# Value groups taken head by head, an earlier end for jobs, and a shorter limit for VectorE's units in an attention and gated-layer kernel

## The chip, the cores and the metric

The kernel runs on one core of a Trainium2 chip. The core has five engines that run their own instruction queues in order and meet through semaphores: TensorE (matmuls; in the profile PE, its weight loads PEld), VectorE (DVE), ScalarE (ACT), GpSimd (POOL) and SyncE (SP), which here issues the DMA transfers. Matmul results go to PSUM, a small memory of banks that hold 512 32-bit numbers in each of 128 partitions; everything else lies in SBUF or in the chip's main memory. The metric is device time of one execution in microseconds (us), lower is better; the time shown is the median of the runs.

## The reference

Two pre-norm blocks follow each other on 2048 rows of 640 numbers: 32-head attention with heads of 20 numbers, then a gated bilinear layer of width 1728. Inputs and output are bf16.

```python
def _A_ref(x, wqkv, wo):
    H = 32; Dh = D // H                    # D = 640, Dh = 20
    qkv = (x @ wqkv).reshape(B, S, 3, H, Dh).transpose(2, 0, 3, 1, 4)
    q, k, v = qkv[0], qkv[1], qkv[2]
    scores = jnp.einsum("bhqd,bhkd->bhqk", q, k) * (Dh ** -0.5)
    p = _softmax(scores, axis=-1)
    o = jnp.einsum("bhqk,bhkd->bhqd", p, v)
    return o.transpose(0, 2, 1, 3).reshape(B, S, D) @ wo
...
def _B_ref(x, w_gate, w_up, w_down):
    g = jnp.einsum("bsd,df->bsf", x, w_gate)
    u = jnp.einsum("bsd,df->bsf", x, w_up)
    return jnp.einsum("bsf,fd->bsd", g * u, w_down)
...
h = x + _A_ref(_layernorm(x), A_wqkv, A_wo)
h2 = h + _B_ref(_layernorm(h), B_w_gate, B_w_up, B_w_down)
```

## The kernel before

**Units and tiles.** Scores are made transposed: keys in the partitions, queries along the row. The smallest piece is a unit: one head, 128 keys, 512 queries (256 in the last passes, "A" and "B"). Four heads form a group; a segment is one group with all its keys for one block of queries (in the first block, a quarter of the keys). The list `segs` (lines 302 to 313) orders the segments, and units of consecutive segments are packed, head after head within a block of 128 keys, into 683 tiles of 1536 columns, three PSUM banks. With 256 queries, two blocks of keys of one head stand next to each other in that list.

**What is done with a tile.** `emit_S` (line 438) writes a tile's scores with TensorE into one of two score buffers of PSUM (`sc`, matmuls of line 448) and has ScalarE write exp of them into one of six buffers `E` (line 461). A score matmul uses 32 rows of TensorE's array, so that four heads lie in four bands of rows. Two tiles later `emit_AV` (line 586) multiplies the exponentials with the values (line 615): each unit writes 32 partitions of one accumulator bank, one column band of the array for each of the four heads, so four units of different heads can run beside each other. Call four such units a step. A column of ones in the values makes the sums for softmax. When a segment's last unit is in, VectorE copies the accumulator (line 626 or 631) and `norm` or `job_norm` divides by the sums, with several small DMAs (lines 530 to 541) or on TensorE.

**VectorE's units.** Where VectorE has time, `emit_x` (line 478) gives the last 512 columns of a tile to it: line 486 reads them from PSUM, and four more operations (lines 496, 497, 498, 491) make an approximate exponential `xe` in integer arithmetic. ScalarE's instruction on that tile is then 1024 columns wide. `x_takes` (line 472) decides it; one of its conditions is that the tile is at least `X_LEAST` tiles ahead of the segment's last. The four operations wait in `x_pieces` until `spare` (line 412) finds room for them, and `put_x` (line 502) then sets the unit at the end of its segment's part of the queue `av_q`. `need_x` makes what is missing before a segment ends.

**How a value group is taken.** `emit_AV` is called once a tile. It counts units at the head of `av_q` that are of one segment and at least two tiles old, eight at most (sixteen narrow ones). With fewer it returns, unless the oldest is over three tiles older than that. It then takes them in the order of the queue.

**Jobs, and the planner that sets the order.** All other work of TensorE (projections, line 278; values, line 292; transposes, line 260; output projection, line 830; gate and up, lines 896 and 914; down, line 951) is cut into jobs, generators that yield after each matmul with its cost. The order of every engine is fixed when the program is built. The main loop (line 1121) goes over the tiles: scores of the tile, one value group, events that are due, then jobs by `run_job` (line 429). It keeps account of times in `at`: TensorE (`pe`), VectorE (`dve`), the job bank `mi`, ScalarE's end (`exp`), the score buffers (`slot`). `S_NS` is the cost of a tile's scores, `S_EXP` the time from scores to the earliest start of the exponential, `SWITCH` what a change of work costs. A value group is charged one step of `w * 5 // 12` ns for every four units. `run_job` is given the time at which TensorE must be free for the next scores; it begins a job only if the job's first part fits, and goes on while the next 216 ns fit, with 60 ns over:

```python
run_job(max(at["exp"] - S_EXP, at["slot"][-2]))
...
while at["pe"] + 216 <= until + 60:
    if step() in (None, NEXT, END):
        break
```

All jobs share one PSUM bank `mi`, which VectorE empties. If there are no jobs, `keep_warm` (line 424) puts two matmuls of no use (line 427) in the gap. What is left of the last block of queries runs in `last_tail` (line 1031) after the last exponential.

**Line numbers.** The changed file is the same up to line 600 and two lines longer from the middle of `emit_AV` on; below, lines are those of before.

Of the kernel before, what the change touches and what calls it, by code (L numbers as in the profile page):

```python
# [27 lines left out]
HPG = 4  # L28
# [3 lines left out]
QB = 512  # L32
# [20 lines left out]
WARM = 58  # L53
LAG = 10
EXP_NS, EXP_END, EXP_COL = 50, 166, 5 / 6
S_NS, S_EXP, SWITCH, LAT = 323, 445, 110, 150
TOL, LEAST = 200, 430
X_LEAST, X_OUT = 4, 6
SHIFT = 1184.0
LOG2E = 1.4426950408889634  # L60
X_UNIT = 128.0
# [10 lines left out]
def kernel(  # L72
# [154 lines left out]
    at = {"pe": 0, "dve": 0, "mi": 0, "acc": 0, "slot": [0, 0], "exp": 0, "av": {}}  # L227
# [88 lines left out]
    for s, (p, g, lo, hi, _) in enumerate(segs):  # L316
        w = PASS[p][2]
# [111 lines left out]
    def run_job(until):  # L429
        if cur["fresh"]:  # L430
            key = urgent[0][0] if urgent else cur["key"] if cur["gen"] is not None else jobs[0][0] if jobs else None
            if key is None or max(at["pe"], at["mi"]) + SWITCH + COST.get(key[0], LEAST) > until:
                return
# [3 lines that stand above are left out]
# [149 lines left out]
    def emit_AV(upto):  # L586
        put_x()
        if not av_q:
            return
        if acc["seg"] is not None and av_q[0][1] != acc["seg"]:  # L590
            need_x(acc["seg"])
            put_x()
        i, s = av_q[0][0:2]
        p, g, lo, hi, kind = segs[s]
        b, c0, w = PASS[p]
        if acc["seg"] != s:
            if at["pe"] < at["acc"] and now["i"] < acc["from"]:
                return
            acc["seg"], acc["left"], acc["n"] = s, (hi - lo) * HPG, [0] * HPG
            acc["t"] = accp.tile([P, QB], F32, name="acc")  # L600
        most = 2 * HPG * QB // w
        ready = 0
        for u in av_q:
            if u[0] > upto or u[1] != s or ready == most:
                break
            ready += 1
        if ready < min(most, acc["left"]) and i > upto - 3:
            return
        for _ in range(ready):
            _, _, kt, j, e = av_q.popleft()  # L610
            if (s, kt, j) in x_last:
                x_live["units"] -= 1
            ensure(("v", kt, g // (NG // 2)))
            h = HPG * g + j
            nc.tensor.matmul(  # L615
                acc["t"][SLOT * j:SLOT * (j + 1), 0:w],
                lhsT=vx[kt][:, VS * h:VS * h + SLOT], rhs=e,
                start=(acc["n"][j] == 0), stop=(acc["n"][j] == hi - lo - 1))
            acc["n"][j] += 1
        acc["left"] -= ready  # L620
        at["pe"] += SWITCH + -(-ready // HPG) * w * 5 // 12
        if acc["left"] == 0:
            dve(690)
            if kind in ("copy", "only"):
                asb = parts[g] if kind == "copy" else nrm.tile([P, QB], F32, name="asb")
                nc.vector.tensor_copy(asb[:, 0:w], acc["t"][:, 0:w])
                if kind == "copy":
                    part[g] = asb
            else:
                asb = part[g]  # L630
                nc.vector.tensor_tensor(asb[:, 0:w], acc["t"][:, 0:w], asb[:, 0:w], ALU.add)
            acc["seg"], acc["from"], at["acc"] = None, now["i"] + 2, at["dve"] + LAT
            if s == FINAL:
                final["asb"] = asb
            elif (p, g) in FAST:
                urgent.append((("nf", p, g), job_norm(s, asb)))
            elif kind in ("only", "last"):
                norm(s, asb)
# [482 lines left out]
    while i < n_tiles or av_q:  # L1121
        now["i"] = i
        if i < n_tiles:
            emit_S(i)
        else:
            while step_x():
                pass
        if i == first_last:
            for g in range(NG):
                ensure(("spill", g))  # L1130
            load_res()
        if i == n_tiles:
            root = small.tile([P, 1], BF16, name="root")
            nc.scalar.activation(root[:], ones[:], ACT.Sqrt)
        emit_AV(i if i >= n_tiles else i - 2 if i >= LAG else i - 4)
        run_events(i)
        if b_seen < NB - 1 and normed(str(b_seen), range(NG)):
            add_tail(b_seen, list(range(TPB)))
            b_seen += 1
        if not a_seen and normed("3", range(SPLIT_G)) and normed("A", range(SPLIT_G, NG)):  # L1140
            add_tail(LAST_B, [0, 1])
            a_seen = True
        if i < n_tiles:
            run_job(max(at["exp"] - S_EXP, at["slot"][-2]))
            idle = max(at["pe"], at["mi"]) + SWITCH + 2 * BANK * EXP_COL / 2
            if i > WARM and cur["gen"] is None and not jobs and idle < at["slot"][-2] + TOL:
                keep_warm()
                at["pe"] = idle
            spare(max(at["pe"], at["slot"][-2]))
        i += 1  # L1150
# [103 lines left out]
```

## Time and profile before

| what | before |
|---|---|
| median of three runs | 979.75 us (979.02 to 979.91) |
| the profiled execution | 976.79 us |
| its span, first to last instruction | 974.9 us |
| mean granted TensorE clock | 0.967 |
| ScalarE busy | 909.5 us |
| TensorE busy | 857.6 us |
| VectorE busy | 589.7 us |

The profile is of one execution. A row of a group gives line, engine, operation, output and input tile, count, then busy time in us and mean length in ns, then the engine's idle time ahead of these instructions with what ended it. Busy time counts overlapping instructions once, so that it can be less than count times mean. The ends of matmuls are modelled: one starts before the other's end. "PEclk" is the share of full clock that TensorE was granted, in tenths. A row of a timeline has start, length, engine, line, and count of a run of like instructions without a gap.

### The profile page before, as it was taken

What the parts mean: (1) busy time and instruction counts of PE and PEld (TensorE: products, weight loads), DVE (VectorE), ACT (ScalarE), POOL (GpSimd) and SP (SyncE); (2) the same over time, 40 slices, a digit from 0 to 9 for tenths busy, and PEclk for the clock granted to TensorE, in tenths of its full rate; (3) what the DMA queues carried; (4) which work ended last, traced back from release to release, by engine and by line L of the source; (5) the groups of instructions that cost most, each with busy time, mean ns of one, the idle gap of its engine ahead of it and who ended that gap; (6) DMA issues with size and microseconds to landing.
All of it is one profiled execution on the core that took longest, in us unless ns stands there. A gap on an engine that the chain in (4) does not pass through costs nothing.

```text
span 974.9 us, 18079 instructions
## 1 busy us (share of the span) xinstructions
PE 857.6 (88%) x7219; PEld 334.2 (34%) x7219; DVE 589.7 (60%) x1181; ACT 909.5 (93%) x719; POOL 65.4 (7%) x163
## 2 busy tenths in 40 slices
PE   7888989888988899988898989988889989988887
PEld 5233232222233222422232223332332334444455
DVE  7665357777777777768777777787562331243232
ACT  6899999999999999999999999999999999999951
POOL 3120011200000000000000000000000000000000
PEclk9999999999987999989997999999998999979999
DMA  6000010100150221041021230001502001202310
GB/s 183 28 2 1 1 37 12 42 17 13 39 156 4 66 67 33 27 149 63 11 64 33 66 88 13 26 27 30 138 2 66 14 13 27 61 8 64 84 34 17
DMA packets 67817, 44.44 MB, mean 46 GB/s; under 512 B 18504, under 2 KB 63404, under 8 KB 67728
## 3 DMA queue, kind: packets, MB, share of 16 engines
q1 hardware_dynamic: 67728, 43.23, 16.0%
q8 instruction: 58, 0.95, 0.4%
q14 instruction: 31, 0.25, 0.1%
HBM read 35.91 MB, written 7.30 MB: 44 GB/s over the span
## 4 chain that ended last, share of the span: by engine, by line
PE 43%; ACT 32%; issue 15%; DVE 9%; DMA 1%; POOL 0%; ACTq 0%; SPq 0%; DVEq 0%; POOLq 0%
ACT E L461 32%; PE sc L448 10%; PE acc L615 8%; PE mi L896 6%; PE mi L278 5%; PE mi L951 5%; PE mi L830 2%; PE f L896 2%; PE mi L292 1%; PE mi L427 1%; PE mi L914 1%; DVE qa L285 1%; PE f L951 1%; DVE u L247 1%; DVE hh L904 1%
## 5 line engine op out<-in xcount | busy, mean ns | idle before, releaser
L461 ACT ACTIVATE E<-sc 128x1536 bf16<-128x1536 f32 (+1 forms) x683 | 892.2, 1411 | 26.0 <-PE sc L448 18.5
L448 PE MATMUL sc<-qa,kT 32*128 32x512 bf16 x1536 | 204.5, 392 | 45.9 <-ACT E L461 41.8
L615 PE MATMUL acc<-E,vx 128*32 128x512 bf16 (+1 forms) x2336 | 186.2, 361 | 0.5 <-ACT E L461 0.5
L448 PEld LDWEIGHTS <-kT 32*128 32x128 bf16 x2432 | 79.5, 91 | 287.1 <-issue 253.4
L486 DVE TENSOR_SCALAR xv<-sc 128x512 f32<-128x512 f32 x95 | 65.5, 690 | 55.3 <-PE sc L448 54.3
L278 PE MATMUL mi<-lnT,wp 128*128 128x512 bf16 x310 | 83.5, 384 | 14.3 <-DVE qa L285 6.4
L547 POOL TENSOR_TENSOR on<-asb,bc 128x512 bf16<-128x512 f32 (+1 forms) x30 | 35.5, 1185 | 726.8 <-DMA bc<-scr 518.0
L448 PE MATMUL sc<-qb,kT 32*128 32x256 bf16 (+1 forms) x896 | 70.9, 300 | 14.5 <-ACT E L461 13.6
L615 PEld LDWEIGHTS <-vx 128*32 128x32 bf16 x2432 | 54.5, 96 | 76.4 <-issue 64.1
L497 DVE SCALAR_TENSOR_TENSOR xt<-xm 128x512 f32<-128x512 int32 x95 | 67.1, 706 | 2.1
L951 PE MATMUL mi<-wd,hh 128*128 128x320 bf16 x378 | 65.9, 301 | 2.3 <-DVE xr L955 2.3
L491 DVE SCALAR_TENSOR_TENSOR xe<-xt,xv 128x512 int16<-128x512 f32 x95 | 67.1, 706 | 1.2
L498 DVE SCALAR_TENSOR_TENSOR xt<-xt,xm 128x512 f32<-128x512 f32 x95 | 66.4, 699 | 2.2
L247 DVE CAST u<-mi 128x512 bf16<-128x512 f32 (+1 forms) x42 | 29.0, 690 | 42.0 <-PE mi L896 41.7
L427 PE MATMUL mi<-kT,ident 128*128 128x512 bf16 x178 | 54.2, 386 | 0.0
L951 PEld LDWEIGHTS <-hh 128*128 128x128 bf16 x448 | 39.3, 97 | 38.8 <-issue 26.2
L896 PE MATMUL mi<-ln2T,wu 128*128 128x512 bf16 (+1 forms) x170 | 48.5, 400 | 3.9 <-DVE hh L904 3.9
L896 PE MATMUL mi<-ln2T,wg 128*128 128x512 bf16 (+1 forms) x170 | 45.7, 381 | 5.9 <-DVE u L247 5.8
L496 DVE TENSOR_SCALAR xm<-xv 128x512 int32<-128x512 int32 x95 | 49.3, 519 | 0.6
L904 DVE TENSOR_TENSOR hh<-mi,u 128x512 bf16<-128x512 f32 (+1 forms) x42 | 28.9, 687 | 32.7 <-PE mi L896 32.4
L278 PEld LDWEIGHTS <-wp 128*128 128x128 bf16 x310 | 26.6, 97 | 57.6 <-issue 41.0
L955 DVE TENSOR_TENSOR xr<-mi,xr 128x320 bf16<-128x320 f32 x27 | 13.1, 485 | 49.0 <-PE mi L951 49.0
(150 smaller groups left out, 637.1 us busy)
## 6 DMA issues: line engine op xcount, KB each, us to landing
bc<-scr SPq DMA_DIRECT2D x100, 64.0 KB
wu<-in_B_w_up_dram SPq DMA_DIRECT2D x20, 320.0 KB
wg<-in_B_w_gate_dram SPq DMA_DIRECT2D x20, 320.0 KB
qsp<-qa SPq DMA_DIRECT2D x8, 384.0 KB
xr<-in_A_x_dram SPq DMA_DIRECT2D x16, 160.0 KB
out_dram<-xr SPq DMA_DIRECT2D x14, 160.0 KB
wd<-in_B_w_down_dram SPq DMA_DIRECT2D x13, 160.0 KB
xs<-in_A_x_dram SPq DMA_DIRECT2D x3, 640.0 KB
```

Source lines behind the costliest of these rows:

```text
L278: nc.tensor.matmul(ps[:], lhsT=wslice(m, g, c), rhs=lnT[:, c, ch * QB:(ch + 1) * QB], start=(c == 0), stop=(c == KT - 1))
L427: nc.tensor.matmul(ps[:], lhsT=ident[:], rhs=kT[0][:, 0:BANK], start=True, stop=True)
L448: nc.tensor.matmul(sc[:, o:o + w], lhsT=kT[g][SLOT * j:SLOT * (j + 1), kt * P:(kt + 1) * P], rhs=q_of(g, b, c0, w)[SLOT * j:SLOT * (j + 1) ...
L461: exps = nc.scalar.activation(e[:, 0:n_act], sc[:, 0:n_act], ACT.Exp, bias=EXP_BIAS, scale=SM_SCALE)
L486: took = nc.vector.tensor_scalar(v[:], ps, X_SCALE, X_BASE, ALU.mult, ALU.max)
L491: nc.vector.scalar_tensor_tensor(e[:], t[:], X_C, v[:], ALU.add, ALU.add)
L496: (480, lambda: nc.vector.tensor_scalar(m[:], v[:].bitcast(I32), 0x7FFF, 0x8000, ALU.bitwise_and, ALU.bitwise_or)),
L497: (700, lambda: nc.vector.scalar_tensor_tensor(t[:], m[:], X_A, m[:], ALU.mult, ALU.mult)),
L498: (700, lambda: nc.vector.scalar_tensor_tensor(t[:], t[:], X_B, m[:], ALU.add, ALU.mult)),
L615: nc.tensor.matmul(acc["t"][SLOT * j:SLOT * (j + 1), 0:w], lhsT=vx[kt][:, VS * h:VS * h + SLOT], rhs=e, start=(acc["n"][j] == 0), stop=(ac ...
L896: nc.tensor.matmul(ps[0:M, 0:n], lhsT=st["w", fp][k][:, c, f2 * P:f2 * P + M], rhs=st["ln2T"][:, c, c0:c0 + n], start=(c == 0), stop=(c == ...
L951: nc.tensor.matmul(ps[:, 0:HALF], lhsT=st["hh"][f][0:K, t * P:(t + 1) * P], rhs=late["Wd"][f][0:K, cs], start=(f == 0), stop=(f == 2 * FP ...
```

## The change

It has three parts.

- The value group is taken from the whole part of the queue that is old enough: at most two units of each head (four of each in the narrow passes), the first of every head, then the second, and so on. The count is the sum over the heads, and the rule on waiting with fewer than the full number is as before.
- `S_EXP` is 500 in place of 445, and `run_job` is given a time that is another 100 ns (`MARGIN`) earlier, if the score buffer is not free even later.
- `X_LEAST` is 3 in place of 4.

```diff
-S_NS, S_EXP, SWITCH, LAT = 323, 445, 110, 150
-TOL, LEAST = 200, 430
-X_LEAST, X_OUT = 4, 6
+S_NS, S_EXP, SWITCH, LAT = 323, 500, 110, 150
+TOL, LEAST, MARGIN = 200, 430, 100
+X_LEAST, X_OUT = 3, 6
...
-        most = 2 * HPG * QB // w
-        ready = 0
+        most, rows = 2 * HPG * QB // w, [[] for _ in range(HPG)]
         for u in av_q:
-            if u[0] > upto or u[1] != s or ready == most:
+            if u[0] > upto or u[1] != s:
                 break
-            ready += 1
+            if len(rows[u[3]]) < most // HPG:
+                rows[u[3]].append(u)
+        ready = sum(len(r) for r in rows)
         if ready < min(most, acc["left"]) and i > upto - 3:
             return
-        for _ in range(ready):
-            _, _, kt, j, e = av_q.popleft()
+        for u in [r[k] for k in range(most // HPG) for r in rows if k < len(r)]:
+            av_q.remove(u)
+            _, _, kt, j, e = u
...
-            run_job(max(at["exp"] - S_EXP, at["slot"][-2]))
+            run_job(max(at["exp"] - S_EXP - MARGIN, at["slot"][-2]))
```

## The prediction

> **What bounds the kernel now.** I read the page first: busy shares, granted clock, the chain of waits that ended last.
>
> ```profile
> span 974.9 us, 18079 instructions
> PE 857.6 (88%) x7219; PEld 334.2 (34%) x7219; DVE 589.7 (60%) x1181; ACT 909.5 (93%) x719; POOL 65.4 (7%) x163
> PEclk9999999999987999989997999999998999979999
> PE 43%; ACT 32%; issue 15%; DVE 9%; DMA 1%; POOL 0%; ACTq 0%; SPq 0%; DVEq 0%; POOLq 0%
> ```
>
> ScalarE has the most work, yet the chain spends 43% of the span on TensorE and 32% on ScalarE. So ScalarE's exponentials (line 461) set the pace, and TensorE makes them late. How much is late follows from the groups by shape and ScalarE's timeline (start, length, count in a merged run).
>
> ```profile
> L461 ACT ACTIVATE E<-sc 128x1536 bf16<-128x1536 f32 x587 | 811.1, 1470 | 23.8 <-PE sc L448 17.5 <-PE acc L615 2.6
> L461 ACT ACTIVATE E<-sc 128x1024 bf16<-128x1024 f32 x96 | 100.8, 1050 | 2.2 <-PE sc L448 1.0
> ...
> 802.97 4.14 ACT L461 ACTIVATE E<-sc 128x1536 bf16<-128x1536 f32 x3
> ...
> 16.02 4.14 ACT L461 ACTIVATE E<-sc 128x1536 bf16<-128x1536 f32 x3 [0.66 <-PE sc L448]
> ...
> 914.71 18.82 ACT L461 ACTIVATE E<-sc 128x1536 bf16<-128x1536 f32 x14
> ```
>
> One exponential lasts 1.47 us, but it overlaps the next: three in a row take 4.14, so one starts (4.14 - 1.47) / 2 = 1.33 after the other. The narrow form, with a bank given to VectorE, lasts 0.42 less, so its spacing is 0.91. Without a stall the 683 would take 587 x 1.33 + 96 x 0.91 = 868.1 us. They run from 16.02 to 914.71 + 18.82 = 933.53, which is 917.5. So **49.4 us are stalls**. The busy column hides this: the idle time shown is 26.0, because an exponential that starts late within the overlap leaves no idle gap.
>
> The list of waits (total us, times, longest) and the chain in order of time (start, length) say whose fault it is.
>
> ```profile
> ACT E L461 <- PE sc L448: 18.5, 38, 1.5
> ...
> ACT E L461 <- PE acc L615: 2.6, 2, 1.7
> ```
>
> ```profile
> 411.29 0.39 PE sc L448 x3
> 411.69 0.75 PE acc L615 x8
> 412.44 0.65 PE mi L951 x4
> 413.09 0.32 PE sc L448 x3
> 413.41 1.19 PE mi L951 x8
> 414.60 0.32 PE sc L448 x3
> 414.93 0.55 PE acc L615 x8
> ...
> 422.44 0.65 PE mi L951 x4
> 423.09 0.37 PE sc L448 x3
> ...
> 423.51 0.94 ACT E L461
> ```
>
> For 12 us the chain goes scores, value products, job matmuls, scores (and, in the lines left out, twice VectorE's copy of a job's bank): TensorE never waits for a free score buffer, and the exponential at 423.51 starts when its scores arrive. I went through all 682 starts: 200 are late by over 20 ns and carry 46.8 of the 49.4 us; the rest are late by 20 ns or less. In none of the 200 had TensorE begun the scores within 0.13 us of the buffer's release. All 200 are thus TensorE behind the written order. 103 of them are late by at most 0.155 us; 24, by over 0.4 us, carry 21.0.
>
> **The change, part by part.** The margin first. S_EXP goes from 445 to 500 and MARGIN takes off 100, so a job must end 0.155 us earlier before the next scores. S_EXP stands for the time from scores to exponential. TensorE's timeline has the scores of that late tile at 423.02, the exponential started at 423.51, so 0.49:
>
> ```profile
> 423.02 0.39 PE L448 MATMUL sc<-qa,kT 32*128 32x512 bf16 x3
> ```
>
> The new 500 is right and 445 was short. If each of the 200 gets its scores 0.155 earlier, 23.7 of the 46.8 remain: 23.1 removed.
>
> Then the value products. A group of eight units ran in queue order; a unit that VectorE took is missing there, so one head can come three times.
>
> ```profile
> 411.62 0.82 PE L615 MATMUL acc<-E,vx 128*32 128x512 bf16 x8
> ...
> 414.86 0.41 PE L615 MATMUL acc<-E,vx 128*32 128x512 bf16 x4
> 415.08 0.38 PE L615 MATMUL acc<-xe,vx 128*32 128x512 bf16 x1
> 415.09 0.39 PE L615 MATMUL acc<-E,vx 128*32 128x512 bf16 x3
> ```
>
> The first group took 0.82; the second ended at 415.09 + 0.39, 0.62 after it began. Three steps against two: 0.20 a step. The planner charges eight units as two steps always, so each long group puts TensorE 0.20 behind. In the order of the built programs, 106 groups need over two steps before and none after; in steps of full width 627 fall to 545, and the groups rise from 262 to 281. That is 82 x 0.20 = 16.4 us of TensorE less, and 19 group changes more at 0.12 each (chain: 0.55 for a group of two steps less 2 x 0.215), 2.3. It counts only where it made scores late: 71 of the 200 have such a group since TensorE's last wait. Less 0.20 on these alone removes 10.5; margin and grouping together leave 18.9 of 46.8, so 27.9 removed. That is the upper end, for the work cut from one tile goes into another. The lower end is grouping alone, 10.5. I take 24, near the upper end, since all 200 fit the mechanism.
>
> In the narrow passes (256 columns, the last quarter of the run) pairs of one head stood next to each other, and now alternate.
>
> ```profile
> 803.47 0.63 PE L615 MATMUL acc<-E,vx 128*32 128x256 bf16 x16
> ```
>
> Sixteen end 0.63 after the first begins. A matmul lasts 0.28, so 0.35 lies between the first and last start: three intervals of 0.11, hence four steps already, as many as after. Nothing is gained. The Trainium skill (TensorE: Matmul & The Clock Gate, Part 3, "What overlaps and what doesn't") says matmuls start strictly in program order; by that the pairs would have made nine steps, and the change would save about 5 x 0.11 in each of 48 groups, 26 us of TensorE. The row shows four, so by the trace the saving is 0.
>
> VectorE's units: X_LEAST 3 and the earlier TensorE times let 102 be taken, not 95. Each takes 0.42 from ScalarE: 7 x 0.42 = 2.9 off.
>
> ```profile
> L497 DVE SCALAR_TENSOR_TENSOR xt<-xm 128x512 f32<-128x512 int32 x95 | 67.1, 706 | 2.1
> L491 DVE SCALAR_TENSOR_TENSOR xe<-xt,xv 128x512 int16<-128x512 f32 x95 | 67.1, 706 | 1.2
> L498 DVE SCALAR_TENSOR_TENSOR xt<-xt,xm 128x512 f32<-128x512 f32 x95 | 66.4, 699 | 2.2
> L486 DVE TENSOR_SCALAR xv<-sc 128x512 f32<-128x512 f32 x95 | 65.5, 690 | 55.3 <-PE sc L448 54.3
> L496 DVE TENSOR_SCALAR xm<-xv 128x512 int32<-128x512 int32 x95 | 49.3, 519 | 0.6
> L615 PE MATMUL acc<-xe,vx 128*32 128x512 bf16 (+1 forms) x96 | 36.4, 390 | 0.0
> ...
> 115.00:690.00 575.00, 513.87 (x3758) 170.43 (x3755) 425.31 (x765) 561.81 (x441) 36.16 (x31) 0.97 0.18 49
> ```
>
> A unit costs VectorE 3.32 us, seven cost 23.2. The last row is a window (TensorE, weight loads, VectorE, ScalarE, GpSimd busy): VectorE is idle for 150 of 575 us there, which covers them. Where the cover fails, an operation stands ahead of a job's copy out of PSUM: 0 to 7 x 0.7 = 4.9 lost. I take 1.0.
>
> New waits. Holding units back for their head keeps an E buffer longer. In the built order four more exponentials (tiles 176, 240, 283, 432) wait for a value group that TensorE gets only after their own scores; behind such an exponential the next score buffer is freed late. The row "ACT E L461 <- PE acc L615" has 2.6 in two such, longest 1.7: 0 to 6.8. Scores and group take 0.32 + 0.55 against the 0.49 that scores alone need, some 0.4 late at most if ScalarE has no lead, so I take 0.3 each, 1.2.
>
> The tail. Jobs end later, and four more matmuls of line 951 come after the last exponential, 1.19 / 8 = 0.15 each: 0.6, or 0 if they lie beside VectorE's copy of the accumulator. I take 0.6. Head and tail are otherwise the same.
>
> DMAs. None is added. On SP's queue three pairs of weight loads, one spill and some stores now stand behind a few transfers of sums and reciprocals that stood behind them; nobody waits for the spill or the stores, and GpSimd's queue is unchanged. The weights are loaded two tiles ahead, and the trace has one wait for them:
>
> ```profile
> L914 PE MATMUL mi<-ln2T,wu 128*128 128x256 bf16 x30 | 4.7, 275 | 3.9 <-DVE hh L921 2.6 <-DMA wu<-in_B_w_up_dram 1.3
> ```
>
> 0 to 3 x 1.3 = 3.9; I take 0, as that one is of the last block and the moved ones are not.
>
> Fillers. The matmul pairs of line 427 fall from 89 to 65, since jobs spread over more tiles.
>
> ```profile
> L427 PE MATMUL mi<-kT,ident 128*128 128x512 bf16 x178 | 54.2, 386 | 0.0
> ...
> 304.00:314.00 10.00, 9.05 (x48) 2.72 (x47) 6.97 (x23) 9.65 (x8) 0.00 (x0) 0.50 0.01 3
> ...
> 300.30:303.70 3.40, 2.09 (x22) 0.77 (x22) 2.79 (x10) 3.40 (x4) 0.00 (x0) 1.00 0.00 0
> ...
> 440.00:450.00 10.00, 8.88 (x65) 2.62 (x63) 7.15 (x12) 10.00 (x9) 0.00 (x0) 1.00 0.20 73
> ```
>
> The first window shows the clock at 0.50 (third column from the end) with TensorE recorded 9.05 of 10 us busy and neither job nor filler in it; just ahead of it TensorE was busy 2.09 of 3.40; the third, with fillers, has 1.00. Over the run 61 us went at half clock, and 8.0 of the stalls lie there, 0.13 per us. If all 24 tiles that lose a filler fell to half clock, 24 x 1.33 x 0.13 = 4.2 would be lost. The stretches without job or filler stand at nearly the same places in both orders, so I take 0. The Trainium skill (same page, Part 1, "The HAM clock gate") halves the clock after an idle window of about 3.4 us. The window ahead of 304 is far from idle and the clock fell, so by that rule no dip would be there, before or after; the row decides against it.
>
> **The sum.** 24 + 2.9 - 1.0 - 1.2 - 0.6 = 24.1 us off. The profiled execution took 976.79 us (span 974.9 and 1.9 around it): 952.7. The median of the runs, 979.75, lies 3.0 above that execution, so by the median **955**, rounded down from 955.7. With all terms at their good ends 27.9 + 2.9 = 30.8, so 949; at their bad ends 10.5 + 2.9 - 4.9 - 6.8 - 0.6 - 3.9 - 4.2 = -7.0, so 987, but these have no reason to fall together.
>
> **The rivals.**
> *Only the grouping pays.* The margin moves a job's matmuls to the next tile, which then ends at its own limit. For: jobs hold most tiles, TensorE is busy 513.87 of 575. Against: 89 pairs of fillers are slack. 10.5 + 2.9 - 2.8 = 10.6 off: 969.
> *Nearly all lateness goes.* Late tiles follow each other, so what is put right once helps the next. Then the stalls at half clock (8.0) and the first ones (3.6 before tile 20) remain, 11.6 of 49.4: 37.8 + 2.9 - 2.8 = 37.9 off, 942. Against: the 24 that are late by over 0.4, which 0.155 doesn't cure.
> *The narrow groups pay after all* (in-order pairs): of the 11.0 us of stalls in those passes the margin leaves 4.6 (the same subtraction there), and these would go as well: 28.7 off, 951. The row of sixteen speaks against it. (This is the rule of order of the Trainium skill's page TensorE: Matmul & The Clock Gate, above.)
> *Slower: TensorE waits for VectorE's units.* They are now taken into a group as soon as their head is short, and up to three tiles from a segment's end; scores stand behind that matmul in the queue. It decides from 24.1 / 102 = 0.24 us a unit on; at 0.35 each, 35.7 lost, the time is 991. Against: idle before "acc<-xe" is 0.0 over 96 now, and a unit must still be two tiles old.
> *It does nothing that shows*: stalls come back elsewhere, 979.
>
> **How the numbers follow.** Forecast 0.70, grouping alone 0.11, nearly all 0.08, narrow groups 0.02, slower 0.06, nothing 0.03. The forecast's own range is 949 to 963, from the good end to half the margin's gain; for 8 in 10 I go from 944, toward the case of 942, to 969, the case of grouping alone. A measurement of this kernel tells about 0.2%, 2 us, from no change: faster 0.91, same 0.03, slower 0.06.
>
> **What would show it.** Right: exponentials' stalls of 22 to 30 us by the same sum; a last exponential that ends near 910; value groups of eight never over 0.65; 103 narrow exponentials; idle before "acc<-xe" at 0. Margin wrong: late tiles still near 200 and most job chains unbroken. Fillers wrong: more than two more zones at 0.50. Wrong altogether: "acc<-xe" or "E <- acc" with over 7 us of idle.

## The result and the profile after

| | before | after |
|---|---|---|
| median of 18 runs | 978.75 us (975.91 to 981.44) | 974.9 us (968.01 to 978.13) |
| ratio of the times | | 0.9959, 95% interval 0.9945 to 0.9973 |
| the profiled execution | 976.79 us | 973.8 us |
| mean granted TensorE clock in it | 0.967 | 0.954 |

The change makes the kernel 0.4% faster: 3.9 us by the medians, where 24.1 were forecast. The time lies above the forecast's range. (The forecast started from 979.75, the median of the first three runs of before; over all 18 it is 978.75.)

The page of the profile after, span, busy shares, granted clock and the engines of the chain that ended last:

```profile
span 972.0 us, 17983 instructions
PE 842.6 (87%) x7171; PEld 323.9 (33%) x7171; DVE 606.6 (62%) x1216; ACT 900.9 (93%) x719; POOL 66.3 (7%) x163
PEclk9999999899988799997997999999887999979999
ACT 40%; PE 33%; issue 15%; DVE 10%; POOL 1%; DMA 1%; SPq 0%; ACTq 0%; POOLq 0%; DVEq 0%
```

TensorE's busy time fell by 15.0 us, and the chain has 33% of the span on it in place of 43%. Most of the 15.0 is the fillers of line 427, which had 54.2 us before:

```profile
L427 PE MATMUL mi<-kT,ident 128*128 128x512 bf16 x130 | 39.8, 388 | 0.0
```

The value groups got shorter too. Their matmuls outside the stretches at half clock, scaled to all units, are 184.3 us of TensorE before and 170.1 after: 14.2 less, which is the 16.4 less 2.3 that were worked out. More time at half clock (below) hides part of it in the busy column. The span fell by 2.9 only, so most of what TensorE was spared came back as waiting. The groups by shape and ScalarE's timeline (line 617 is line 615 of before) give the stalls by the prediction's own sum:

```profile
L461 ACT ACTIVATE E<-sc 128x1536 bf16<-128x1536 f32 x580 | 803.7, 1514 | 22.6 <-PE sc L448 17.3 <-PE acc L617 3.7
L461 ACT ACTIVATE E<-sc 128x1024 bf16<-128x1024 f32 x103 | 113.2, 1099 | 7.8 <-PE sc L448 6.9 <-PE acc L617 0.5
```

```profile
15.54 10.89 ACT L461 ACTIVATE E<-sc 128x1536 bf16<-128x1536 f32 x8 [0.66 <-PE sc L448]
...
880.00 48.60 ACT L461 ACTIVATE E<-sc 128x1536 bf16<-128x1536 f32 x36 [0.34 <-PE sc L448]
```

Without a stall, 580 x 1.33 + 103 x 0.91 = 865.1 us. They run from 15.54 to 928.60, which is 913.1, so 48.0 us are stalls, against 49.4 before. The forecast had 22 to 30. The list of waits shows of what kind they are now:

```profile
ACT E L461 <- PE sc L448: 24.2, 29, 4.8
ACT E L461 <- PE acc L617: 4.2, 4, 1.7
```

Before, 38 waits for scores had 18.5 us and the longest was 1.5. Now 29 have 24.2 and the longest is 4.8. Sorted by how late each exponential starts after the one ahead of it (in us; the spacings are taken to the nanosecond, so the totals differ a little from the sum above):

| stalls of | before | after |
|---|---|---|
| up to 0.06 | 4.4 | 3.3 |
| 0.06 to 0.15 | 6.3 (61 tiles) | 3.8 (39) |
| 0.15 to 0.4 | 17.7 (73) | 10.6 (48) |
| over 0.4 | 21.0 (24) | 30.5 (24) |
| total | 49.4 | 48.2 |
| tiles late by over 0.02 | 200 | 136 |

The small stalls shrank by 10.7 us, and the large ones grew by 9.5. Two make that up, 5.04 us behind the exponential that starts at 183.18 and 4.39 us behind the one at 53.50; before, the largest of all was 1.88.

**The stall at 183.** The timeline of after there (start, length, engine, line, operation, count, idle time ahead with what ended it):

```profile
180.64 1.27 POOL L547 TENSOR_TENSOR on<-asb,bc 128x512 bf16<-128x512 f32 x1 [25.29 <-DMA bc<-scr]
181.11 5.65 DVE L496 TENSOR_SCALAR xm<-xv 128x512 int32<-128x512 int32 x1
...
181.84 4.63 POOL L774 MEMSET wo<- 128x640 bf16 x8
...
186.68 0.73 DVE L285 TENSOR_SCALAR kT<-mi,one_row 128x512 bf16<-128x512 f32 x1
...
187.47 1.44 PE L278 MATMUL mi<-lnT,wp 128*128 128x512 bf16 x3 [4.70 <-DVE kT L285]
...
188.84 0.61 PE L448 MATMUL sc<-qa,kT 32*128 32x512 bf16 x3
...
189.55 1.02 ACT L461 ACTIVATE E<-sc 128x1024 bf16<-128x1024 f32 x1 [4.83 <-PE sc L448]
```

Line 496, one of the four operations of VectorE's unit, has a median of 0.42 us, and lasts up to 1.5 where it begins inside another line 547. Here it began while GpSimd was in line 547 and stood until GpSimd's eight memsets (the clearing of the output weights' tiles in `load_wo`, line 774) were over. Behind it on VectorE waited the copy of a projection out of the job bank, behind that the next job on TensorE, behind that the scores. The same place before:

```profile
181.36 0.42 DVE L496 TENSOR_SCALAR xm<-xv 128x512 int32<-128x512 int32 x1
181.79 1.27 POOL L547 TENSOR_TENSOR on<-asb,bc 128x512 bf16<-128x512 f32 x1 [28.11 <-DVE xm L496]
181.81 1.80 DVE L497 SCALAR_TENSOR_TENSOR xt<-xm 128x512 f32<-128x512 int32 x1
183.00 4.64 POOL L772 MEMSET wo<- 128x640 bf16 x8
...
186.99 0.92 DVE L496 TENSOR_SCALAR xm<-xv 128x512 int32<-128x512 int32 x1
```

Before, line 496 ended just ahead of line 547, and the next one came near the end of the memsets. It was line 497 that began inside line 547, and it lasted 1.80 in place of 0.69, but ended well ahead of the memsets' end. The change moved VectorE's unit by 0.9 us against GpSimd's work: from 0.43 ahead of line 547's start to 0.47 behind it.

**The stall at 53.5.** TensorE's timeline of after, and behind it that of before at the same tile (the 27th):

```profile
52.35 0.39 PE L448 MATMUL sc<-qa,kT 32*128 32x512 bf16 x3 [0.63 <-ACT E L461]
...
53.46 0.85 PE L292 MATMUL mi<-wv,lnT 128*128 128x320 bf16 x5
54.95 0.84 PE L292 MATMUL mi<-wv,lnT 128*128 128x320 bf16 x5 [0.64 <-DVE vx L247]
56.38 1.24 PE L278 MATMUL mi<-lnT,wp 128*128 128x512 bf16 x5 [0.58 <-DVE vx L247]
57.55 0.39 PE L448 MATMUL sc<-qa,kT 32*128 32x512 bf16 x2
58.75 0.40 PE L448 MATMUL sc<-qa,kT 32*128 32x512 bf16 x4 [0.81 <-DVE kT L285]
```

```profile
54.33 1.25 PE L278 MATMUL mi<-lnT,wp 128*128 128x512 bf16 x5
55.51 0.39 PE L448 MATMUL sc<-qa,kT 32*128 32x512 bf16 x2
56.42 0.39 PE L448 MATMUL sc<-qa,kT 32*128 32x512 bf16 x4 [0.52 <-DVE kT L285]
```

The third of this tile's scores (the first of the x4) waits for the copy of a projection of keys (line 278), which must be made by then, whether it fits or not (`ensure` in `emit_S`). Before, that projection alone stood ahead. With the margin jobs were put off, and now two value jobs (line 292) and the projection stand between two tiles' scores, each waiting for VectorE to empty the one job bank.

### The profile page after: what moved, and what is told of

Its sections match the earlier page's. It is cut to its first block, busy times and chain, and to the rows that moved or that the text cites. A ratio compares the mean times of both kernels' runs of the same rounds, so it can differ in the third digit from the quotient of the medians.

```text
span 972.0 us, 17983 instructions
## 1 busy us (share of the span) xinstructions
PE 842.6 (87%) x7171; PEld 323.9 (33%) x7171; DVE 606.6 (62%) x1216; ACT 900.9 (93%) x719; POOL 66.3 (7%) x163
## 4 chain that ended last, share of the span: by engine, by line
ACT 40%; PE 33%; issue 15%; DVE 10%; POOL 1%; DMA 1%; SPq 0%; ACTq 0%; POOLq 0%; DVEq 0%
ACT E L461 40%; PE sc L448 8%; PE acc L617 6%; PE mi L898 4%; PE mi L278 4%; PE mi L953 3%; PE f L898 2%; PE mi L832 1%; DVE st L182 1%; PE mi L292 1%; DVE xm L496 1%; PE f L953 1%; DVE kT L285 1%; DVE u L247 1%; DVE xt L498 1%
## 5 line engine op out<-in xcount | busy, mean ns | idle before, releaser
L461 ACT ACTIVATE E<-sc 128x1536 bf16<-128x1536 f32 (+1 forms) x683 | 883.3, 1451 | 30.4 <-PE sc L448 24.2
L448 PE MATMUL sc<-qa,kT 32*128 32x512 bf16 x1536 | 208.2, 396 | 56.0 <-ACT E L461 47.5
L617 PE MATMUL acc<-E,vx 128*32 128x512 bf16 (+1 forms) x2330 | 175.2, 365 | 0.4 <-ACT E L461 0.4
L486 DVE TENSOR_SCALAR xv<-sc 128x512 f32<-128x512 f32 x102 | 70.2, 688 | 39.4 <-PE sc L448 38.2
L498 DVE SCALAR_TENSOR_TENSOR xt<-xt,xm 128x512 f32<-128x512 f32 x102 | 72.7, 713 | 2.1
L497 DVE SCALAR_TENSOR_TENSOR xt<-xm 128x512 f32<-128x512 int32 x102 | 72.0, 706 | 2.4
L491 DVE SCALAR_TENSOR_TENSOR xe<-xt,xv 128x512 int16<-128x512 f32 x102 | 71.1, 697 | 1.1
L617 PEld LDWEIGHTS <-vx 128*32 128x32 bf16 x2432 | 45.2, 96 | 69.4 <-issue 68.8
L898 PE MATMUL mi<-ln2T,wu 128*128 128x512 bf16 (+1 forms) x170 | 49.4, 400 | 5.9 <-DVE hh L906 5.7
L278 PEld LDWEIGHTS <-wp 128*128 128x128 bf16 x310 | 26.0, 97 | 59.3 <-issue 43.5
L832 PE MATMUL mi<-wo,on 128*128 128x320 bf16 x224 | 39.1, 307 | 1.5 <-DVE xr L836 1.3
L617 PE MATMUL acc<-xe,vx 128*32 128x512 bf16 x102 | 39.4, 405 | 0.8 <-DVE xe L491 0.8
```

Of the source, the lines that this page charges most:

```text
L278: nc.tensor.matmul(ps[:], lhsT=wslice(m, g, c), rhs=lnT[:, c, ch * QB:(ch + 1) * QB], start=(c == 0), stop=(c == KT - 1))
L448: nc.tensor.matmul(sc[:, o:o + w], lhsT=kT[g][SLOT * j:SLOT * (j + 1), kt * P:(kt + 1) * P], rhs=q_of(g, b, c0, w)[SLOT * j:SLOT * (j + 1) ...
L461: exps = nc.scalar.activation(e[:, 0:n_act], sc[:, 0:n_act], ACT.Exp, bias=EXP_BIAS, scale=SM_SCALE)
L486: took = nc.vector.tensor_scalar(v[:], ps, X_SCALE, X_BASE, ALU.mult, ALU.max)
L491: nc.vector.scalar_tensor_tensor(e[:], t[:], X_C, v[:], ALU.add, ALU.add)
L497: (700, lambda: nc.vector.scalar_tensor_tensor(t[:], m[:], X_A, m[:], ALU.mult, ALU.mult)),
```

## The experiments

My theory after reading the two traces: groups and X_LEAST give what was forecast, and the margin loses it again through the order it makes, at these two places. The rivals: the half clock, which rose from 63.6 us of the span to 89.5, costs it; or the grouping doesn't pay. Twelve kernels were run. Times are medians; "before" is the kernel before on the same chip in the same series.

| run | median us | before | ratio, 95% interval |
|---|---|---|---|
| e4_memset_spread | 976.06 | 978.17 | 0.9984 (0.996 to 1.0008) |
| e5_fill_waits | 973.72 | 978.17 | 0.996 (0.9934 to 0.9986) |
| e6_early_as_before | 979.32 | 978.17 | 1.0005 (0.9984 to 1.0027) |
| e8_all | 977.88 | 978.17 | 1.0001 (0.9971 to 1.003) |
| k1_memset_vector | 970.49 | 978.05 | 0.9912 (0.9881 to 0.9942) |
| f1_no_margin | 968.24 | 978.05 | 0.9895 (0.9871 to 0.9918) |
| k7_no_groups | 989.65 | 978.05 | 1.0105 (1.0077 to 1.0133) |
| k3_charge_all | 965.11 | 978.05 | 0.9873 (0.9848 to 0.9897) |
| p1_margin_late | 966.52 | 977.1 | 0.9889 (0.9851 to 0.9927) |
| p0_no_margin_late | 967.9 | 977.1 | 0.9912 (0.9884 to 0.994) |
| p4_charge_fill | 960.63 | 977.1 | 0.983 (0.9793 to 0.9867) |
| g3_xleast_alone | 975.26 | 977.1 | 0.9985 (0.9966 to 1.0005) |

Margin or grouping alone upon the kernel before were not tried. In several of the orders that follow a value group would, with six `E` buffers, wait for an exponential that itself waits for that group; these have seven, and where a run has seven this is said.

**e4: the memsets one to a tile.**

```diff
-        for g in range(NG):
+        def one(g):
             nc.gpsimd.memset(wo[g][:], 0.0)
-        for g in range(NG):
             for j in range(HPG):
                 ...
+        for g in range(NG):
+            later(g, lambda g=g: one(g))
```

> The changed kernel, with GpSimd's eight memsets of wo (and the loads behind each) put one to a tile instead of all eight at once; nothing else moves on TensorE, VectorE and ScalarE. Theory A (the margin and the groups gain as reckoned, and the gain is lost in a few places: one VectorE operation of 5.65 us beside the memsets, more time at half clock, and an early tile): the longest operation of line 496 falls from 5.65 to under 2 us, the gap of 5.0 us between exponentials near 183 us goes, and the time falls by 5 to 7 us, to 968 to 970. Theory B (the lateness is set by VectorE having more to do, and comes back elsewhere): the block goes but the time falls by less than 2 us.

The edit didn't do what it was made for. The timeline of this run:

```profile
183.83 1.27 POOL L547 TENSOR_TENSOR on<-asb,bc 128x512 bf16<-128x512 f32 x1 [25.21 <-DMA bc<-scr]
184.16 5.80 DVE L496 TENSOR_SCALAR xm<-xv 128x512 int32<-128x512 int32 x1
...
185.04 4.64 POOL L774 MEMSET wo<- 128x640 bf16 x8
```

The memsets were issued over eight tiles, but GpSimd's queue stood in order behind line 547, which waits for a DMA, and when that came they ran in one go as before. Line 496 stood 5.80 us. Nothing on the price follows, except that the same meeting gives the same stall again (5.18).

**e5: filler matmuls in every tile in which no job ran.**

```diff
+            pe_was = at["pe"]
             run_job(max(at["exp"] - S_EXP - MARGIN, at["slot"][-2]))
 ...
-            if i > WARM and cur["gen"] is None and not jobs and idle < at["slot"][-2] + TOL:
+            if i > WARM and cur["fresh"] and at["pe"] == pe_was and idle < at["slot"][-2] + TOL:
```

> The changed kernel, with the pair of filler matmuls (line 427) in every tile in which no job ran, not only when no job is left: 108 pairs for 65. Theory A: time at half clock falls from 92 us to under 20, the stalls inside such stretches from 20 us to under 8 (the 5 us beside the memsets stay), and the time falls by 7 to 11 us, to 964 to 968. Theory B: the half clock goes, but the fillers make scores late in their place and the time falls by less than 3 us, or rises.

The groups of this run have 216 filler matmuls in place of 130, and the time at half clock fell from 89.5 to 45.1 us:

```profile
L427 PE MATMUL mi<-kT,ident 128*128 128x512 bf16 x216 | 67.1, 393 | 3.5 <-DVE on L580 1.8 <-DVE sums_all L564 0.7 <-DVE ln2T L247 0.7
```

The ratio is that of the change itself (0.996 and 0.9959), the medians differ by 1.2 us, and the stalls are 46.8 against 48.2. The spans of the two profiled executions differ by 3.0, as the tail is shorter too (below). So 44 us less of half clock, bought with 86 more filler matmuls, are worth 0 to 3 us, and the expected 7 to 11 didn't come. That is not the price of the half clock alone, since fillers and the order that they make can cost something too: in the two traces the stalls fall by 4.9 us between tiles 87 and 511 and rise by 3.1 behind them. The runs of one kernel point to a higher price. Take as time at half clock twice what the granted clock lacks of 1, times the span: the 48 runs of before in the series of this table had 58 to 80 us of it, and in each of the three series a run is about 0.3 us longer for each us more (0.28 to 0.31). By that figure the 26 us that after has more than before would be some 8 us; that the clock is the cause there was not tested. The rival thus can't account for all of the 20 us that are missing, and for a part of them it stays open.

**e6: the job limit of before up to tile 86.** Both places lie ahead of tile 125.

```diff
-            run_job(max(at["exp"] - S_EXP - MARGIN, at["slot"][-2]))
+            run_job(max(at["exp"] - (S_EXP + MARGIN if i > 86 else 445), at["slot"][-2]))
```

> The changed kernel, with the old limit for jobs (445, no margin) up to tile 86, where projections are due before scores. Theory A: the gap of 4.4 us near 53 us falls to 1.6 as before, and the time by 2 to 3 us, to 972. Theory B: no change within 1 us. The orders after tile 86 can shift, so the collision with the memsets may go or come with it, worth 5 us.

A miss. `emit_S` still reckons with `S_EXP` 500 when it sets `at["exp"]`, so the planner's times stayed other than before (p1 below changes that place too), and the projection still came late: the stall near 55 us was 4.10, that at the memsets 5.19.

**e8: the edits of e4, e5 and e6 together.**

```diff
-            nc.gpsimd.memset(wo[g][:], 0.0)
+            later(g, lambda g=g: one(g))
 ...
-            run_job(max(at["exp"] - S_EXP - MARGIN, at["slot"][-2]))
+            run_job(max(at["exp"] - (S_EXP + MARGIN if i > 86 else 445), at["slot"][-2]))
 ...
+            if i > WARM and cur["fresh"] and at["pe"] == pe_was and idle < at["slot"][-2] + TOL:
```

> The three edits of the other runs together (memsets one to a tile, fillers in every tile without a job, old limit up to tile 86) on the changed kernel. Theory A: 15 to 20 us off, 955 to 960, which is what the prediction reckoned with for the change alone. Theory B: 970 or more.

Since neither place was mended (3.62 us near 57 and 5.19 near 191), it shows no gain either. It says nothing on the price of the two.

**k1: the memsets on VectorE, one to a tile.** This takes away what line 496 met. (The expectation says that GpSimd's queue had nothing to wait for in e4; the row of line 547 above shows its wait, 25.21 us.)

```diff
+        def one(g):
+            nc.vector.memset(wo[g][:], 0.0)
             for j in range(HPG):
                 ...
+        for g in range(NG):
+            later(g, lambda g=g: one(g))
```

> The changed kernel with the eight memsets of wo on VectorE, one to a tile, in place of GpSimd. (One to a tile on GpSimd changed nothing there: its queue had nothing to wait for, and the eight still ran in 4.64 us in one go beside the operation of line 496, now 5.80 us.) Theory A (the block beside the memsets is a loss of its own, 5.0 us and 1 to 1.5 in the half clock that follows): line 496 has no operation over 2 us, the gap at tile 121 goes, 5 to 6.5 us off, 968 to 970. Theory B (what is won at one place comes back at the next): under 2 us off.

The view of line 496 (shortest, median and longest in ns) of after, then of this run:

```profile
L496 DVE TENSOR_SCALAR xm<-xv x102: 365/419/5650, 141.5 to 699.3; 128x512 int32<-128x512 int32 x102
```

```profile
L496 DVE TENSOR_SCALAR xm<-xv x102: 364/419/1496, 146.1 to 695.7; 128x512 int32<-128x512 int32 x102
```

The longest is 1.50 in place of 5.65, the stall is gone, and the median is 974.9 - 970.49 = 4.4 us below that of after (in ratios 0.0047 of 978, 4.6 us). The eight memsets cost VectorE 2.6 us. So the meeting was worth some 4.4 of the 5.0 that it shows; these are four runs, from 968.18 to 972.76, and the interval of the ratio is 3 us to either side. The profiled execution, 972.49, is one of the longer ones: all its stalls are 46.7 against 47.9 by the same sum, only 1.2 less. Up to tile 86, where the edit has not yet acted, it has 4.5 us more of them than after, with four stretches at half clock ahead of 100 us where after has none; from tile 87 on it has 5.8 less. The stall of tile 27 remained, at 3.98.

**f1: the change without its margin.** Groups and X_LEAST 3 stay.

```diff
-S_NS, S_EXP, SWITCH, LAT = 323, 500, 110, 150
+S_NS, S_EXP, SWITCH, LAT = 323, 445, 110, 150
 ...
-            run_job(max(at["exp"] - S_EXP - MARGIN, at["slot"][-2]))
+            run_job(max(at["exp"] - S_EXP, at["slot"][-2]))
```

> The changed kernel with 445 and no margin again; groups by head and X_LEAST 3 stay. The prediction's reckoning (each late tile gains 0.155 us from the margin): the margin was worth 13 us, so 985 to 988. Theory C (late tiles come in runs, the 200 of before in 91 of them; the delay grows within a run by what the planner doesn't charge, and the margin shortens a run once, not each tile of it): the margin was worth at most 91 runs, 11 us, less what it lost at tile 27 (2.8) and where its order met the memsets (5.0): within 4 us of the changed kernel, 971 to 979, with about 90 runs of late tiles for 73.

Without the margin the kernel is faster: 968.24, 9.8 us below before. That is what the rival "only the grouping pays" worked out, 10.6 and 969. So the margin costs 974.9 - 968.24 = 6.7 us as it was made (6.3 by the ratios, 4.9 between the two profiled spans), and the half clock isn't why: f1 has 86.2 us of it, after 89.5. Neither of the two places is there (the largest stall is 2.26). GpSimd's memsets are where they were, and line 496 met them another way:

```profile
181.97 4.91 POOL L774 MEMSET wo<- 128x640 bf16 x8
...
184.46 0.69 DVE L496 TENSOR_SCALAR xm<-xv 128x512 int32<-128x512 int32 x1
```

It began after the memsets had, and lasted 0.69.

**k7: the change without its grouping**, with seven `E` buffers.

```diff
-        most, rows = 2 * HPG * QB // w, [[] for _ in range(HPG)]
+        most = 2 * HPG * QB // w
+        ready = 0
 ...
-        for u in [r[k] for k in range(most // HPG) for r in rows if k < len(r)]:
-            av_q.remove(u)
-            _, _, kt, j, e = u
+        for _ in range(ready):
+            _, _, kt, j, e = av_q.popleft()
```

> The changed kernel with groups in queue order again (seven E buffers in place of six, without which this order can't be built); margin and X_LEAST 3 stay. The prediction's reckoning: the grouping was worth 8 to 11 us: 983 to 986. Rival: it was worth nothing, since the scores wait for jobs and not for groups: 973 to 976, with long groups (0.8 us) in the timeline but no more late tiles.

It is slower than both, and 14.8 us slower than after. Line 496 meets the memsets here too (5.33), so this difference isn't in that. The rival that the grouping doesn't pay falls.

**p1: the margin from tile 87 on, in both places of the planner**, with k1's memsets and seven `E` buffers. Up to tile 86 the limits are those of before.

```diff
-        start = max(at["exp"], begin + S_EXP)
+        start = max(at["exp"], begin + (S_EXP if i > 86 else 445))
 ...
-            run_job(max(at["exp"] - S_EXP - MARGIN, at["slot"][-2]))
+            run_job(max(at["exp"] - (S_EXP + MARGIN if i > 86 else 445), at["slot"][-2]))
```

> The changed kernel with the planner of before (445, no margin) up to tile 86, memsets of wo on VectorE, and seven E buffers; the margin and 500 act from tile 87 on. Theory C (the margin costs where it meets the memsets, 4.4 measured, and where it makes a due projection late at tile 27, 2.5 to 2.9): 966 to 969, like the changed kernel without any margin (968), and the gap near 54 us is 1.5 as before. Rival (the margin costs everywhere): stays at 970 or more.

As expected. Tile 27 waits for one projection again, with 1.2 us of idle time, and the median is 4.0 us below k1's (2.2 by ratios, as before was 0.95 lower in this series). It has one unit more and a seventh buffer besides, and the margin is off for all of the first 86 tiles, so the second place, with whatever else the margin did there, is worth some 2 to 4 us; the two intervals overlap. In the traces tiles 20 to 30 have 5.5 us of stalls after and 1.5 in p1.

**p0: the same with no margin** (99 units in place of 103 on VectorE).

```diff
-TOL, LEAST, MARGIN = 200, 430, 100
+TOL, LEAST, MARGIN = 200, 430, 0
```

> The same with MARGIN 0 (500 alone from tile 87 on; 99 units for VectorE for 103, worth 1.7). The prediction's reckoning (0.100 off each of some 130 late tiles): 10 us or more slower than with the margin. Theory C (a run of late tiles is shortened once; 70 to 80 runs, and part of what is won is lost in waits for VectorE's copies): 1 to 5 us slower, 968 to 973, the 1.7 included.

At 967.9 it is 1.4 us above p1, and its four units less would be 4 x 0.42 = 1.7, all of that. With both places out of the way, the last 100 ns of margin are worth nothing that shows. Against f1 p1 gains 1.7 us (0.6 by ratios). So the margin, clear of its accidents, is worth some 2 us by the medians; the intervals allow a few us more, and p1 differs from f1 in the buffers and the memsets too.

**k3: the planner is told what a job costs the scores behind it**, with k1's memsets, e5's fillers and seven `E` buffers; the margin stays everywhere. Where the late tiles that are left come from is seen in TensorE's timeline of after:

```profile
294.65 0.39 PE L448 MATMUL sc<-qa,kT 32*128 32x512 bf16 x3
294.98 0.45 PE L832 MATMUL mi<-wo,on 128*128 128x320 bf16 x2
295.55 0.39 PE L448 MATMUL sc<-qa,kT 32*128 32x512 bf16 x3
295.88 0.40 PE L617 MATMUL acc<-E,vx 128*32 128x512 bf16 x4
296.10 0.38 PE L617 MATMUL acc<-xe,vx 128*32 128x512 bf16 x1
296.11 0.39 PE L617 MATMUL acc<-E,vx 128*32 128x512 bf16 x3
296.42 0.99 PE L832 MATMUL mi<-wo,on 128*128 128x320 bf16 x6
297.35 0.39 PE L448 MATMUL sc<-qa,kT 32*128 32x512 bf16 x3
```

The group of eight takes two steps and its 0.54 (295.88 to 296.42) are just what the planner charges, 0.11 + 2 x 0.213. But the two job matmuls take from 294.98 to 295.55, 0.57, where the charge is 0.11 + 2 x 0.136 = 0.38. The six that follow a break take 0.93; a job that goes on is charged no switch, so 0.82. Over all such intervals in which TensorE sets the pace at full clock, the median error was 0.106 us before (0.212 with a full-width group) and is 0.033 after (0.011).

```diff
-        begin = max(at["pe"], at["slot"][-2])
+        begin = max(at["pe"] + 100 * at.pop("job", 0), at["slot"][-2])
```

(`at["job"]` is set to 1 in `step` wherever a job's cost is added to `at["pe"]`.)

> The changed kernel with three edits: the planner charges TensorE 100 ns more for scores that follow a job (the trace has 0.23 from the last job matmul's start to the scores where the planner has 0.136), memsets on VectorE, fillers in every tile without a job; seven E buffers. Theory C: with the charge the errors no longer add up over a run: late tiles fall under 100 and stalls under 30 us, 955 to 963 (98 units for VectorE in place of 102 cost 1.7 of it). Theory B: 968 or more.

Charge, fillers and the seventh buffer bring 965.11, 5.4 us below k1, though a stall for scores of 4.4 us is still there. Late tiles are 96 in place of 136.

**p4: p1 with the charge from tile 87 on and the fillers**, six `E` buffers.

```diff
-        begin = max(at["pe"], at["slot"][-2])
+        begin = max(at["pe"] + 100 * at.pop("job", 0) * (i > 86), at["slot"][-2])
 ...
-            if i > WARM and cur["gen"] is None and not jobs and idle < at["slot"][-2] + TOL:
+            if i > WARM and cur["fresh"] and at["pe"] == pe_was and idle < at["slot"][-2] + TOL:
```

> The same as the run with the margin from tile 87 on, with six E buffers, the charge of 100 ns for scores that follow a job (from tile 87 on too), and fillers in every tile without a job; 99 units for VectorE. Theory C: errors no longer add up, 957 to 962, below the 965 of the run that had charge and margin from the start. Rival (what the charge won was the fillers' and the memsets' doing): 965 or more.

960.63, the best of all: 16.5 us below before and 5.9 below p1. Its page, groups and waits (line 462 is line 461 of after):

```profile
span 959.0 us, 17960 instructions
...
L462 ACT ACTIVATE E<-sc 128x1536 bf16<-128x1536 f32 x583 | 809.6, 1555 | 18.0 <-PE sc L449 12.6 <-PE acc L618 4.5
...
ACT E L462 <- PE sc L449: 13.1, 19, 1.5
```

The longest wait for scores is 1.5 again, there are 19 in place of 29, and the stalls are 32.1 us. By e5 the fillers are 1 to 3 us of the 5.9; charge, buffers and fillers were not taken apart further.

**g3: X_LEAST 3 alone upon the kernel before**, seven `E` buffers, 102 units.

```diff
-X_LEAST, X_OUT = 4, 6
+X_LEAST, X_OUT = 3, 6
```

> The kernel before with X_LEAST 3 alone (and seven E buffers): 102 units for VectorE for 95. The prediction's term: 7 x 0.42 = 2.9 off, 975 to 976. Rival: the seven units bring groups of three steps and put VectorE's copies back, so nothing is left, 978 or more.

1.8 us below before, with an interval from 3.3 less to 0.5 more. It allows the 2.9 less 1.0 of the forecast and can't tell it from nothing. The seventh buffer is in that figure; by itself, or in the other orders, it was not tried.

## Why the prediction was wrong

**The bound.** ScalarE's exponentials made late by TensorE: right, before and after. TensorE's scores still end most of the waits.

**The margin: the step that failed.** The prediction put it so: "If each of the 200 gets its scores 0.155 earlier, 23.7 of the 46.8 remain: 23.1 removed", and took 24 with the grouping, "near the upper end, since all 200 fit the mechanism"; the grouping alone being 10.5, the margin stood in the sum with 13.5. Measured, it lost 6.7 us (f1). Between the traces of f1 and after, stalls over 0.4 us grew from 23.4 to 30.5, and the tail by 2.5. Three things were wrong in that sentence.

- *It counted each late tile by itself.* The 200 lie in 91 runs of late tiles, through which TensorE never waits for a free buffer. A job that stops earlier gives 0.155 where such a run begins. The errors that follow are new ones: the chain that the prediction shows from 411 to 423 is one such run. Counted once a run, the same subtraction gives 11.4, not 23.1.
- *Even that didn't come.* From f1 to after, stalls of up to 0.4 us went from 21.2 to 17.7, 3.5 less. Between p0 and p1 the last 100 ns make no difference that the time shows. Why the rest of the 11.4 stayed away was not traced tile by tile; the jobs' uncharged 0.1 to 0.2 is one reason that the rows show, and k3 and p4, which charge it, have fewer late tiles (96 and 108).
- *Its lower bound was nothing.* "The lower end is grouping alone" gave the margin a price of 0 at worst. But a margin moves every later instruction, on VectorE as well, and two moves were bad: line 496 into GpSimd's memsets (4.4 us by k1) and a due projection into a pile of three jobs (2 to 4 us by p1 against k1, less cleanly). The rows for the first were in the profile of before: line 496's operation of 0.92 beside the memsets, and eight memsets of 4.64 us in one run. The prediction read the queues for moves of order and found GpSimd's "unchanged"; it didn't ask what VectorE's moved operations would meet there.

**The grouping** was right by its total: 10.5 and the units' 2.9 less 2.8 were worked out as 10.6 together, f1 has 9.8. The sizes inside the sum are less sure: in f1's trace the stalls are 44.7, 4.7 less than before, where 10.5 less 1.0 and 1.2 would be 8.3, while its time at half clock is 23 us more. With the margin in place the grouping is worth more, 14.8 (k7, with a seventh buffer). TensorE's value work fell by 14.2 where 14.1 were worked out, and the groups rose from 262 to 281; of the groups of eight with their own record 109 of 202 lasted over 0.65 before, and 15 of 156 after, 14 of them because of the half clock (1.04) and one as it waited for values. That the narrow groups would give nothing fits too: sixteen still take 0.62 at 923 us.

**The units**: 102 and 103 narrow exponentials, as forecast. The idle time ahead of the products with `xe` is 0.8 us, not 0. The price of VectorE's work (1.0) can't be seen apart in f1's sum; it didn't cover the one meeting with GpSimd.

**The new waits for value groups** were sized at 1.2: the row has 4.2 in four waits against 2.6 in two, 1.6 more. The size was right, the places in part: of the four tiles named, 176 and 432 wait, for 0.7 together, and the rest is at tile 219, which waited before already and waits 0.8 longer.

**The tail** was sized at 0.6. From the last exponential's end to the span's it is 41.4 before and 43.4 after. A window of after shows where (busy time of TensorE, weight loads, VectorE, ScalarE, GpSimd; then granted clock):

```profile
940.00:944.00 4.00, 3.69 (x19) 2.66 (x19) 0.42 (x1) 2.23 (x7) 0.00 (x0) 0.57 0.75 205
```

Gate and up of the last rows run there without a pause, and 3.4 us of it at half clock would be 1.7 of the 2.0. Most executions fit that: without such a zone the tail is 40.9 in f1, 41.4 in p0, 41.5 in e4 and 41.8 in e5, and with one 43.2 to 43.5 (after, k1, e6, p1, g3); k3 and p4, in orders of their own, have 43.7 and 44.5 without one. As g3 has no margin, the zone isn't shown to be the change's doing.

**The clock.** "The stretches without job or filler stand at nearly the same places": nine zones at half clock became eleven, and longer, 89.5 us in place of 63.6. The step failed; what that cost isn't settled. The forecast's price of 0.13 per us would make 3.4 of the 26 us more. In e5 44 us less, with the fillers that it took, won 0 to 3 us and 1.4 of stalls; the spread over runs of one kernel, 0.3 per us, would make some 8.

**The rivals.** "Only the grouping pays" (0.11) comes within a microsecond of f1, the kernel without the margin. The forecast itself, and "nearly all lateness goes", fell with the margin. "Stalls come back elsewhere" (0.03) was the nearest to what the whole change does, with 979 against 974.9. That the margin itself could lose, and so eat what the grouping wins, was in none of them.

## What to carry to other kernels

A margin in a planned order is worth at most what it saves at the start of each chain of late work, once, not at every late instruction. Look first for the charge that is wrong (here 0.1 us behind each job): p4, which mends it from tile 87 on, was the fastest, though it wasn't taken apart from its fillers. Any shift of the plan moves all engines against each other: look for what is long, unplanned and off the critical path (here eight memsets in a row) and for work with a fixed due time, and price a meeting with them as a loss before giving the shift a lower bound of zero.

## What the runs showed of the hardware

A VectorE operation can stand still through a whole run of GpSimd instructions, and which operation it is matters. Line 496 (integers, SBUF to SBUF) began inside line 547, with the memsets right behind it, in six runs (after, e4, e5, e6, e8, k7), and in each stood 5.3 to 5.8 us, until 0.3 us past the last of the eight memsets. In f1 and before it began inside the memsets and lasted 0.69 and 0.92; in f1 it took a turn between two memsets, the sixth of which lasted 0.90 in place of 0.63. In k1, where line 547 runs from 185.70 for 1.28 us with no memset behind it, line 496 began at 185.95 and ended 0.28 past its end:

```profile
185.95 1.31 DVE L496 TENSOR_SCALAR xm<-xv 128x512 int32<-128x512 int32 x1
```

The three other operations of the unit (lines 497, 498, 491) are held by line 547 too, but not by the memsets. Where one of them began inside line 547 with the memsets right behind (before, f1, g3), it ended 0.55 past the end of line 547, with the first memsets running, after 1.64 to 1.80 us; inside the memsets they take their usual 0.67 to 0.69. Operations that read PSUM, such as line 285 (0.74 to 0.75 there), were not held by either.

The Trainium skill (SBUF — State Buffer, "SBUF: two separate sides") says that VectorE's two-port operations and GpSimd share a pair of ports, which whoever starts first holds for the whole instruction. That fits the wait for line 547 and the short ones inside the memsets. It doesn't say that the one waiting may be passed over by eight further instructions, which is what line 496 shows in these six; why it got no turn there, and got one in f1, stays open.
